# The second FFN's hi/lo split, cut into two steps: three plain slots, then four formed slots

## Chip, core and metric

The kernel runs on one core of a Trainium2 chip. The metric is the device time of one execution in microseconds (us). Beside the time of whole runs there is one profiled execution, with a trace of every engine: PE (TensorE matmuls) and PEld (its weight loads), DVE (VectorE), ACT (ScalarE), POOL (GpSimd), and SP, which only issues DMAs here.

## What is computed

```python
def _attn_ref(q, k, v, tau):                # 1 x 6016 x 256 each
    qn = q / (norm(q, axis=1) + 1e-06);  kn = k / (norm(k, axis=1) + 1e-06)
    s = kn.transpose(0, 2, 1) @ qn / tau    # 256 x 256
    a = softmax(s)
    return v @ a                            # 6016 x 256
def _moe_ref(x, w_in, w_out):               # FFN 1, d_model 256, d_ff 2048
    h = x @ w_in
    return (h * np.cos(h)) @ w_out
def _moe2_ref(x, w_in, w_out):              # FFN 2, the same sizes
    h = x @ w_in
    return (h * (1.0 / (1.0 + np.exp(-h)))) @ w_out     # silu(h)
# result: _moe2_ref(_moe_ref(_attn_ref(...)))
```

## The kernel before

**Stages.** After the attention's 256 x 256 matrix has been folded into FFN 1's first weights, the kernel is two FFNs, one after the other. Tokens go in 12 blocks (four of 512, then eight of 496), the hidden width of 2048 in 8 pairs of 128 rows. A *unit* is one FFN, one block b and one pair m: FFN 1 has 96 units, and then FFN 2 has 96. In names such as `h2_5_1` the numbers are FFN, block and pair.

**Precision.** Every matmul operand is kept as two parts, hi (the value rounded to fp32r) and lo (the rest), and a product takes three passes: hi·hi, hi·lo, lo·hi (`PASSES`).

**A unit of FFN 2.** PE computes h in 12 matmuls (L365) into one of two PSUM tiles `h`. ACT writes silu(h) into slots 0 to 3 of a tile `t` (L381): the 2 x 2 quarters of the block, two hidden halves by two token halves, each 128 x n/2. The second product is done by Strassen's scheme (Winograd's form), with seven products in place of eight. It needs four more slots, which DVE forms in `emit_cos` (L396 writes slots 4 and 5, L399 slot 6, L400 slot 7). `emit_split` then makes hi and lo of slots 1 to 7, one ACT copy (L414) and one DVE subtraction (L415). PE's second product is `emit_o2`: 21 matmuls (L465), seven products by three passes, into two PSUM tiles `o`.

```python
PRODUCTS = {"P1": (1, 1), "P2": (3, 3), "P3": (7, 2), "P4": (2, 7), "P5": (4, 4), "P6": (6, 6), "P7": (5, 5)}
BANKS = {
    "P1": (0, 0, 0), "P6": (0, 0, 1), "P7": (0, 1, 0), "P4": (0, 1, 1),
    "P5": (1, 0, 0), "P3": (1, 0, 1), "P2": (1, 1, 0),
}
```

The second number of a product is the slot of `t` that it reads, and the order of `BANKS` is the order in which PE works: P1 (slot 1), P6 (6), P7 (5), P4 (7) go into the first `o` tile, P5 (4), P3 (2), P2 (3) into the second. P1, P3 and P2 read plain slots, the others formed ones.

**End of a block.** `emit_out` takes a finished block out of PSUM: one ACT copy (L488, called q1 here) and seven DVE additions (L486). The third addition is the last that reads the first `o` tile, the seventh the last that reads the second. There are only two `o` tiles and a block holds both, so the next block's first product waits for these additions.

**Order.** The order on each engine is the order of the code, unit after unit (the loop at L528). Iteration i emits h of unit i, its silu, its forms, its split, and then the second product of unit i − 2 (`LAG = 2`); the second product of a block's last pair comes before the split (`early_o`), and with it `emit_out`, so that the additions of a block stand on DVE between the forms and the subtraction of the next block's unit m = 1. The tiles `t`, `hi`, `lo` and `h` have two buffers each: hi and lo of unit u can be written once the second product of unit u − 2 has read them.

Of the kernel before, what the change touches and what calls it, by code (L numbers as in the profile page):

```python
# [9 lines left out]
F32 = mybir.dt.float32  # L10
# [4 lines left out]
AF = mybir.ActivationFunctionType  # L15
ALU = mybir.AluOpType
# [22 lines left out]
NU = NS - 1  # L39
# [20 lines left out]
def attention_then_two_ffns(ctx: ExitStack, tc: tile.TileContext, qk, vT, tau, w_in1, w_out1, w_in2, w_out2, outT):  # L60
# [6 lines left out]
    nc = tc.nc  # L67
# [168 lines left out]
    for g, n in enumerate(GROUPS):  # L236
        c0 = sum(GROUPS[:g])
        t = ep.tile([P, GMAX, 2, C], F32, tag="qk", name=f"qk{g}", bufs=8)
# [47 lines left out]
    for a in range(CH):  # L286
        nc.vector.scalar_tensor_tensor(
            out=E[:, a], in0=S[:, a, :C], scalar=rk[:, a : a + 1], in1=rq, op0=ALU.mult, op1=ALU.mult
# [80 lines left out]
    def emit_first(u, hp):  # L369
        L, b, m = u  # L370
        n = BLOCKS[b][1]
        t = sc.tile([P, NS, HB], F32, tag="t", name=f"t{L}_{b}_{m}")
        if L == 1:
            t = t.rearrange("p s c -> p (s c)")[:, : 2 * TB].rearrange("p (s n) -> p s n", s=2)
            k = t.bitcast(I32)[:, :, :n]
            nc.scalar.activation(k, hp[:, :, :n], AF.Copy, scale=1.0 / TWO_PI, bias=0.25)  # L376
            nc.vector.scalar_tensor_tensor(  # L377
                out=t[:, :, :n], in0=k, scalar=-TWO_PI, in1=hp[:, :, :n], op0=ALU.mult, op1=ALU.add
            )
        else:  # L380
            nc.scalar.activation(  # L381
                t[:, :4].rearrange("p (s j) c -> p s j c", s=2)[:, :, :, : n // 2],
                hp[:, :, :n].rearrange("p s (j c) -> p s j c", j=2),
                AF.Silu,
            )
        return t
# [15 lines left out]
    def emit_split(u, t):  # L402
        L, b, m = u
        n = BLOCKS[b][1]
        hi = sc.tile([P, NU, HB], F32R, tag="hi", name=f"hi{L}_{b}_{m}")
        lo = sc.tile([P, NU, HB], F32R, tag="lo", name=f"lo{L}_{b}_{m}")
        if L == 1:
            hi, lo = [
                x.rearrange("p s c -> p (s c)")[:, : 2 * TB].rearrange("p (s n) -> p s n", s=2) for x in (hi, lo)
            ]  # L410
            w, z, x = hi[:, :, :n], lo[:, :, :n], t[:, :, :n]
        else:
            w, z, x = hi[:, :, : n // 2], lo[:, :, : n // 2], t[:, 1:, : n // 2]
        nc.scalar.activation(w, x, AF.Copy)  # L414
        nc.vector.tensor_tensor(out=z, in0=x, in1=w.bitcast(F32), op=ALU.subtract)  # L415
        return hi, lo

    def emit_o1(u, parts):
# [109 lines left out]
    for i in range(len(units) + LAG):  # L528
        if i < len(units):
# [13 lines left out]
            t = emit_first(u, hp)  # L543
        if pend is not None:
            parts[pend[0]] = emit_split(units[pend[0]], pend[1])
            pend = None
# [7 lines left out]
        if i < len(units):  # L554
            if L == 1:
                pend = (i, t)
            else:
                parts[i] = emit_split(u, t)
            if (L, b) == (1, 0):
                WO1.load()  # L560
                WO1.decode()
                if m >= NPAIR - 2:
                    WI2.load()
            if (L, b) in ((1, 1), (1, 2)) and m % 2 == 0:
                WI2.decode()
                WI2.load()
            if (L, b) == (1, 2) and m >= NPAIR - 2:
                WO2.load()
            if (L, b) in ((1, 3), (1, 4), (1, 5), (1, 6)) and m % 4 == 0:
                WO2.decode()  # L570
                WO2.load()
            if m == 2:
                if L == 1 and 1 <= b < NB - 1:
                    load_v(b + 1)
                elif (L, b) == (1, NB - 1):
                    load_x2(0)
                elif L == 2 and b < NB - 1:
                    load_x2(b + 1)
            if (L, b) == (1, NB - 1) and m % 2 == 1:
                fetch_wo2(HELD + m // 2)  # L580
# [32 lines left out]
```

## Time and profile before

| what | value |
|---|---|
| time, median of 3 runs | 1136.78 us (1136.54 to 1137.22) |
| the profiled execution: time, and its span | 1136.23 us, 1134.5 us |
| busy in the span: PE, PEld, DVE, ACT, POOL | 1093.4, 933.5, 835.9, 612.1, 207.0 us |
| mean granted TensorE clock | 0.995 |
| FFN 2, from its first h matmul to the end | 600.46 to 1134.5 us |

The span runs from the first to the last instruction; the time of the execution has 1.7 us more around it. "Idle before" in a row is the time that an engine stood still ahead of that instruction, with the instruction that ended it. [...]

### The profile page before, as it was taken

What the parts mean: (1) busy time and instruction counts of PE and PEld (TensorE: products, weight loads), DVE (VectorE), ACT (ScalarE), POOL (GpSimd) and SP (SyncE); (2) the same over time, 40 slices, a digit from 0 to 9 for tenths busy, and PEclk for the clock granted to TensorE, in tenths of its full rate; (3) what the DMA queues carried; (4) which work ended last, traced back from release to release, by engine and by line L of the source; (5) the groups of instructions that cost most, each with busy time, mean ns of one, the idle gap of its engine ahead of it and who ended that gap; (6) DMA issues with size and microseconds to landing.
All of it is one profiled execution on the core that took longest, in us unless ns stands there. A gap on an engine that the chain in (4) does not pass through costs nothing.

```text
span 1134.5 us, 14054 instructions
## 1 busy us (share of the span) xinstructions
PE 1093.4 (96%) x5724; PEld 933.5 (82%) x5724; DVE 835.9 (74%) x914; ACT 612.1 (54%) x582; POOL 207.0 (18%) x173
## 2 busy tenths in 40 slices
PE   8888999999999999999999999999999999999997
PEld 7746788888888888888888888988988988988986
DVE  6899988877887766677666677677677667676675
ACT  6555666656656555555554444544444444445443
POOL 2268565543543311011000000000000000000000
PEclk9999999999999999999999999999999999999999
DMA  9812222303133011011063011010110110110100
GB/s 356 283 47 83 94 75 93 111 19 106 52 135 108 38 49 54 1 55 54 1 235 106 1 57 52 5 55 18 38 54 9 47 54 1 55 55 1 55 18 19
DMA packets 31792, 77.97 MB, mean 69 GB/s; under 512 B 2416, under 2 KB 14704, under 8 KB 31728
## 3 DMA queue, kind: packets, MB, share of 16 engines
q1 hardware_dynamic: 31584, 76.83, 19.8%
q8 instruction: 45, 0.74, 0.3%
q10 hardware_dynamic: 144, 0.25, 0.1%
q14 instruction: 19, 0.16, 0.0%
HBM read 53.08 MB, written 23.99 MB: 68 GB/s over the span
## 4 chain that ended last, share of the span: by engine, by line
PE 75%; DVE 18%; ACT 5%; issue 1%; DMA 1%; SPq 0%; ACTq 0%; DVEq 0%
PE h L365 38%; PE o L425 22%; PE o L465 15%; DVE lo L415 6%; ACT hi L414 4%; DVE acc L256 2%; DVE t L396 2%; DVE t L399 1%; DVE t L400 1%; PE pw L323 1%; DMA qk<-qk_dram 1%; DVE t L377 1%; DVE q L486 1%; DVE t L393 1%; DVE wv_wo L129 1%
## 5 line engine op out<-in xcount | busy, mean ns | idle before, releaser
L415 DVE TENSOR_TENSOR lo<-t,hi 128x992 fp32r<-128x992 f32 (+3 forms) x192 | 324.0, 1687 | 156.7 <-ACT hi L414 156.7
L414 ACT ACTIVATE hi<-t 128x992 fp32r<-128x992 f32 (+3 forms) x192 | 260.0, 1354 | 267.3 <-DVE t L400 236.6
L465 PE MATMUL o<-hi,wo 128*128 128x248 f32 (+1 forms) x1344 | 241.7, 282 | 18.0 <-DVE ob L486 17.1
L465 PEld LDWEIGHTS o<-hi,wo 128*128 128x128 f32 x1344 | 212.3, 191 | 29.6 <-issue 21.6
L365 PE MATMUL h<-xhi,wa 128*128 128x496 f32 (+1 forms) x768 | 206.2, 391 | 3.0 <-DVE wa L331 3.0
L425 PE MATMUL o<-hi,wo 128*128 128x496 f32 (+1 forms) x768 | 205.9, 390 | 0.0
L377 DVE SCALAR_TENSOR_TENSOR t<-t,h 128x992 f32<-128x992 int32 (+1 forms) x96 | 115.0, 1198 | 106.5 <-ACT t L376 106.2
L465 PE MATMUL o<-lo,wo 128*128 128x248 f32 (+1 forms) x672 | 188.5, 281 | 2.6 <-DVE lo L415 2.6
L376 ACT ACTIVATE t<-h 128x992 int32<-128x992 f32 (+1 forms) x96 | 96.9, 1009 | 157.5 <-PE h L365 153.4
L365 PEld LDWEIGHTS h<-xhi,wa 128*128 128x128 f32 x768 | 144.3, 188 | 34.5 <-issue 4.3
L425 PEld LDWEIGHTS o<-hi,wo 128*128 128x128 f32 x768 | 144.4, 188 | 30.5
L392 ACT ACTIVATE t<-t,half_pi 128x992 f32<-128x992 f32 (+1 forms) x96 | 109.1, 1137 | 55.8 <-DVE t L377 55.8
L465 PEld LDWEIGHTS o<-lo,wo 128*128 128x128 f32 x672 | 128.0, 190 | 3.0 <-DVE lo L415 3.0
L425 PE MATMUL o<-lo,wo 128*128 128x496 f32 (+1 forms) x384 | 119.2, 392 | 6.2 <-DVE lo L415 6.2
L393 DVE TENSOR_TENSOR t<-h,t 128x992 f32<-128x992 f32 (+1 forms) x96 | 115.1, 1199 | 7.1 <-ACT t L392 1.2
L365 PE MATMUL h<-x2lo,wi_hi 128*128 128x496 f32 (+1 forms) x384 | 119.5, 393 | 0.0
L365 PE MATMUL h<-x2hi,wi_lo 128*128 128x496 f32 (+1 forms) x384 | 118.9, 391 | 0.0
L365 PE MATMUL h<-x2hi,wi_hi 128*128 128x496 f32 (+1 forms) x384 | 118.8, 391 | 0.0
L365 PE MATMUL h<-xlo,wa 128*128 128x496 f32 (+1 forms) x384 | 118.4, 390 | 0.0
L381 ACT ACTIVATE t<-h 128x992 f32<-128x992 f32 (+1 forms) x96 | 95.0, 989 | 2.9 <-PE h L365 2.8
L425 PEld LDWEIGHTS o<-lo,wo 128*128 128x128 f32 x384 | 71.6, 188 | 23.7 <-DVE lo L415 9.2
L365 PEld LDWEIGHTS h<-x2lo,wi_hi 128*128 128x128 f32 x384 | 72.3, 188 | 15.3
(88 smaller groups left out, 912.7 us busy)
## 6 DMA issues: line engine op xcount, KB each, us to landing
qk<-qk_dram SPq DMA_DIRECT2D x22, 512.0 KB, 7.2
raw_wo<-w_out_dram SPq DMA_DIRECT2D x16, 512.0 KB, 3.9
wo_dram<-stage SPq DMA_DIRECT2D x6, 896.0 KB, 4.5
wo<-wo_dram SPq DMA_DIRECT2D x6, 896.0 KB, 5.5
raw_w<-w_in_dram SPq DMA_DIRECT2D x8, 512.0 KB, 7.6
raw_wi<-w_in_dram SPq DMA_DIRECT2D x8, 512.0 KB, 3.8
vraw<-vT_dram SPq DMA_DIRECT2D x8, 496.0 KB, 5.4
xshi<-yhi SPq DMA_DIRECT2D x8, 496.0 KB, 4.0
```

The source lines that it names most:

```text
L256: nc.vector.tensor_tensor(out=acc[:, :n], in0=acc[:, :n], in1=sq[:, :n], op=ALU.add)
L365: nc.tensor.matmul(hp[:, s, :n], lhsT, rhs, start=(i == 0), stop=(i == len(todo) - 1))
L376: nc.scalar.activation(k, hp[:, :, :n], AF.Copy, scale=1.0 / TWO_PI, bias=0.25)
L377: nc.vector.scalar_tensor_tensor(out=t[:, :, :n], in0=k, scalar=-TWO_PI, in1=hp[:, :, :n], op0=ALU.mult, op1=ALU.add)
L381: nc.scalar.activation(t[:, :4].rearrange("p (s j) c -> p s j c", s=2)[:, :, :, : n // 2], hp[:, :, :n].rearrange("p s (j c) -> p s j c", ...
L392: nc.scalar.activation(t[:, :, :n], t[:, :, :n], AF.Sin, bias=half_pi)
L393: nc.vector.tensor_tensor(out=t[:, :, :n], in0=hp[:, :, :n], in1=t[:, :, :n], op=ALU.mult)
L396: nc.vector.tensor_tensor(out=t[:, 4:6, :c], in0=t[:, 0:1, :c].to_broadcast([P, 2, c]), in1=t[:, 1:3, :c], op=ALU.subtract)
L414: nc.scalar.activation(w, x, AF.Copy)
L415: nc.vector.tensor_tensor(out=z, in0=x, in1=w.bitcast(F32), op=ALU.subtract)
L425: nc.tensor.matmul(o[:, e, :n], wo1_at(i, f)[:, e * P : (e + 1) * P], parts[k][:, s, :n], start=(f == 0 and (i, k) == PASSES[0]), stop=(f ...
L465: nc.tensor.matmul(o[t][:, k, j, :c], wo2[m][:, w, wa_ - 1], parts[x][:, xb - 1, :c], start=(m == 0 and i == 0 and j == 0), stop=(m == NPA ...
```

## The change

For FFN 2 `emit_split` no longer works on seven slots at once. It emits a copy and a subtraction of slots 1 to 3, which silu writes, and then a copy and a subtraction of slots 4 to 7, which the forms write. The operations, their engines and their operands are otherwise the same; FFN 1 has one step as before. Line numbers after it move by three (L414 and L415 are L417 and L418, L465 is L468, L486 and L488 are L489 and L491).

```diff
@@ emit_split
         else:
-            w, z, x = hi[:, :, : n // 2], lo[:, :, : n // 2], t[:, 1:, : n // 2]
-        nc.scalar.activation(w, x, AF.Copy)
-        nc.vector.tensor_tensor(out=z, in0=x, in1=w.bitcast(F32), op=ALU.subtract)
+            some = [
+                (hi[:, a:z, : n // 2], lo[:, a:z, : n // 2], t[:, 1 + a : 1 + z, : n // 2]) for a, z in ((0, 3), (3, NU))
+            ]
+        for w, z, x in some:
+            nc.scalar.activation(w, x, AF.Copy)
+            nc.vector.tensor_tensor(out=z, in0=x, in1=w.bitcast(F32), op=ALU.subtract)
         return hi, lo
```

ACT before, at the border from block 4 to block 5 (units 5_1 to 5_3), with the engines whose semaphores an instruction waits for; "Activation" is ACT itself:

```order
L381 ACTIVATE t2_5_1_6063<-h2_5_1_6050 128x4x248 [waits PE_49]
L488 ACTIVATE q4_6089<-o2_4_0_5769 128x248 [waits PE_49]
L414 ACTIVATE hi2_5_1_6100<-t2_5_1_6063 128x7x248 [waits DVE_49,PE_49,Activation_49]
L381 ACTIVATE t2_5_2_6117<-h2_5_2_6104 128x4x248 [waits PE_49]
L414 ACTIVATE hi2_5_2_6122<-t2_5_2_6117 128x7x248 [waits DVE_49,PE_49,Activation_49]
L381 ACTIVATE t2_5_3_6166<-h2_5_3_6153 128x4x248 [waits PE_49]
```

The same place of ACT with the change:

```order
L381 ACTIVATE t2_5_1_6145<-h2_5_1_6132 128x4x248 [waits PE_49]
L491 ACTIVATE q4_6171<-o2_4_0_5839 128x248 [waits PE_49]
L417 ACTIVATE hi2_5_1_6182<-t2_5_1_6145 128x3x248 [waits PE_49,Activation_49]
L417 ACTIVATE hi2_5_1_6182<-t2_5_1_6145 128x4x248 [waits DVE_49]
L381 ACTIVATE t2_5_2_6201<-h2_5_2_6188 128x4x248 [waits PE_49]
L417 ACTIVATE hi2_5_2_6206<-t2_5_2_6201 128x3x248 [waits PE_49,Activation_49]
L417 ACTIVATE hi2_5_2_6206<-t2_5_2_6201 128x4x248 [waits DVE_49]
L381 ACTIVATE t2_5_3_6252<-h2_5_3_6239 128x4x248 [waits PE_49]
```

One copy has become two. The copy of three slots no longer waits for DVE; it still waits for PE, the last matmul that reads the buffer (unit u − 2). The copy of four waits for DVE alone, for the L400 of its own unit.

DVE with the change, at the same border (the seven L489 are `emit_out`'s additions); before, one subtraction `128x7x248`, waiting for ACT, stood in the place of the two L418 rows, and the other rows were the same:

```order
L489 TENSOR_TENSOR q4_6171<-q4_6171,o2_4_0_5839 128x248 [waits Activation_49]
L489 TENSOR_TENSOR q4_6171<-q4_6171,o2_4_0_5839 128x248 [waits DVE_49]
L489 TENSOR_TENSOR ob4_6172<-q4_6171,o2_4_0_5839 128x248 [waits DMAHW7_49,DVE_49]
L489 TENSOR_TENSOR ob4_6172<-q4_6171,o2_4_1_5840 128x248 [waits PE_49]
L489 TENSOR_TENSOR q4_6171<-q4_6171,o2_4_1_5840 128x248 [waits DVE_49]
L489 TENSOR_TENSOR ob4_6172<-q4_6171,o2_4_1_5840 128x248 [waits DVE_49]
L489 TENSOR_TENSOR ob4_6172<-q4_6171,o2_4_1_5840 128x248
L418 TENSOR_TENSOR lo2_5_1_6183<-t2_5_1_6145,hi2_5_1_6182 128x3x248 [waits Activation_49]
L418 TENSOR_TENSOR lo2_5_1_6183<-t2_5_1_6145,hi2_5_1_6182 128x4x248 [waits Activation_49]
L396 TENSOR_TENSOR t2_5_2_6201<-t2_5_2_6201 128x2x248 [waits Activation_49]
L399 TENSOR_TENSOR t2_5_2_6201<-t2_5_2_6201 128x248 [waits DVE_49]
```

Nothing has moved past anything else on DVE: forms, additions, then the two subtractions in place of one.

PE with the change, the first eight of the 21 matmuls of unit 5_1's second product; before, the rows that wait were only the first and the third:

```order
L468 MATMUL o2_5_0_6216<-hi2_5_1_6182,wo2_1_530 128x248 [waits Activation_49]
L468 MATMUL o2_5_0_6216<-hi2_5_1_6182,wo2_1_530 128x248
L468 MATMUL o2_5_0_6216<-lo2_5_1_6183,wo2_1_530 128x248 [waits DVE_49]
L468 MATMUL o2_5_0_6216<-hi2_5_1_6182,wo2_1_530 128x248 [waits Activation_49]
L468 MATMUL o2_5_0_6216<-hi2_5_1_6182,wo2_1_530 128x248
L468 MATMUL o2_5_0_6216<-lo2_5_1_6183,wo2_1_530 128x248 [waits DVE_49]
L468 MATMUL o2_5_0_6216<-hi2_5_1_6182,wo2_1_530 128x248 x2
```

PE's matmuls and their order are as before; P6, the second product, now waits by itself for the copy and the subtraction of the four slots.

## Rows read from the trace of the kernel before

**Rows 1.** The page's part 4, shares of the chain that ended last.
```profile
PE 75%; DVE 18%; ACT 5%; issue 1%; DMA 1%; SPq 0%; ACTq 0%; DVEq 0%
```

**Rows 2.** Windows: stretch, its length, busy time per engine, clock, DMA share, GB/s.
```profile
160.00:605.96 445.96, 445.96 (x1965) 368.91 (x1964) 332.83 (x294) 266.45 (x268) 124.07 (x101) 1.00 0.22 74
...
702.47:706.56 4.09, 4.09 (x21) 4.09 (x22) 3.99 (x7) 1.34 (x2) 0.00 (x0) 0.58 0.46 137
...
833.38:876.31 42.93, 41.19 (x264) 37.21 (x265) 29.62 (x40) 20.58 (x18) 0.00 (x0) 1.00 0.11 36
```

**Rows 3.** Who waited for whom, 640 to 1130 us: total, times, longest.
```profile
ACT hi L414 <- DVE t L400: 221.6, 79, 3.7
DVE lo L415 <- ACT hi L414: 143.8, 79, 2.1
...
PE o L465 <- DVE ob L486: 17.1, 10, 1.8
```

**Rows 4.** DVE's timeline at a block's border: start, us, instruction, idle before.
```profile
825.18 0.67 DVE L396 TENSOR_TENSOR t<-t 128x496 f32<-128x496 f32 x1
...
826.34 0.42 DVE L400 TENSOR_TENSOR t<-t 128x248 f32<-128x248 f32 x1
828.56 1.97 DVE L415 TENSOR_TENSOR lo<-t,hi 128x1736 fp32r<-128x1736 f32 x1 [1.80 <-ACT hi L414]
830.44 0.67 DVE L396 TENSOR_TENSOR t<-t 128x496 f32<-128x496 f32 x1
...
831.93 0.85 DVE L486 TENSOR_TENSOR q<-q,o 128x248 f32<-128x248 f32 x2
832.82 0.73 DVE L486 TENSOR_TENSOR ob<-q,o 128x248 f32<-128x248 f32 x2
...
834.03 0.73 DVE L486 TENSOR_TENSOR ob<-q,o 128x248 f32<-128x248 f32 x2
```

**Rows 5.** ACT's timeline at the same border.
```profile
826.87 1.66 ACT L414 ACTIVATE hi<-t 128x1736 fp32r<-128x1736 f32 x1 [2.72 <-DVE t L400]
828.43 0.98 ACT L381 ACTIVATE t<-h 128x992 f32<-128x992 f32 x1
829.30 0.37 ACT L488 ACTIVATE q<-o 128x248 f32<-128x248 f32 x1
```

**Rows 6.** PE's timeline in FFN 2: first matmuls of first and second products.
```profile
614.25 0.40 PE L465 MATMUL o<-hi,wo 128*128 128x256 f32 x2
...
635.37 0.41 PE L465 MATMUL o<-hi,wo 128*128 128x256 f32 x2
...
790.41 0.47 PE L465 MATMUL o<-hi,wo 128*128 128x248 f32 x2 [1.60 <-DVE ob L486]
...
823.66 0.61 PE L365 MATMUL h<-x2hi,wi_hi 128*128 128x496 f32 x2
...
826.38 0.39 PE L465 MATMUL o<-hi,wo 128*128 128x248 f32 x2
...
828.76 0.61 PE L365 MATMUL h<-x2hi,wi_hi 128*128 128x496 f32 x2
...
833.38 0.47 PE L465 MATMUL o<-hi,wo 128*128 128x248 f32 x2 [1.74 <-DVE ob L486]
...
1090.98 0.47 PE L465 MATMUL o<-hi,wo 128*128 128x248 f32 x2 [1.74 <-DVE ob L486]
```

**Rows 7.** Timelines of ACT and DVE at FFN 1's last unit.
```profile
604.38 1.02 ACT L414 ACTIVATE hi<-t 128x992 fp32r<-128x992 f32 x1
...
605.43 1.19 DVE L415 TENSOR_TENSOR lo<-t,hi 128x992 fp32r<-128x992 f32 x1 [2.89 <-ACT hi L414]
```

**Rows 8.** The kernel's end, PE and ACT.
```profile
1116.72 0.39 PE L465 MATMUL o<-hi,wo 128*128 128x248 f32 x2
...
1125.85 0.38 PE L465 MATMUL o<-lo,wo 128*128 128x248 f32 x1 [1.51 <-DVE lo L415]
...
1127.93 0.38 ACT L488 ACTIVATE q<-o 128x248 f32<-128x248 f32 x1 [4.13 <-PE o L465]
```

More of the change, by code (lines that the diff above doesn't have):

```diff
@@ L410, in emit_split @@
             ]
-            w, z, x = hi[:, :, :n], lo[:, :, :n], t[:, :, :n]
+            some = [(hi[:, :, :n], lo[:, :, :n], t[:, :, :n])]
         else:
-            w, z, x = hi[:, :, : n // 2], lo[:, :, : n // 2], t[:, 1:, : n // 2]
-        nc.scalar.activation(w, x, AF.Copy)
-        nc.vector.tensor_tensor(out=z, in0=x, in1=w.bitcast(F32), op=ALU.subtract)
+            some = [
[4 more added lines that the diff above has]
+            nc.vector.tensor_tensor(out=z, in0=x, in1=w.bitcast(F32), op=ALU.subtract)
         return hi, lo
```

## Prediction

> **What bounds the kernel now.** I began with PE by stage. In FFN 1 (160 to 606 us) PE is busy 445.96 of 445.96 us; in a block of FFN 2 it is busy 41.19 of 42.93 us [rows 2]. FFN 1 has no idle time of PE to give, and the change leaves it alone, so only FFN 2 is looked at. There PE is busy but not the bound: the chain that ended last runs 18% through DVE and 5% through ACT [rows 1], and the waits of FFN 2 show a pair that hand work to each other, ACT's copy waiting for DVE's forms (221.6 us) and DVE's subtraction waiting for the copy (143.8 us) [rows 3]. Such waits cost nothing by themselves. They matter if their loop is longer than PE's unit.
>
> PE's unit: from the h product at 823.66 us to the next at 828.76 is 5.10 us, 2.72 for h and 2.38 for the second product [rows 6]. The loop of DVE and ACT: forms from 825.18 to 826.76 (1.58), handover 0.11, copy 1.66, handover 0.03, subtraction 1.97, and the next forms begin at 830.44 [rows 4, 5]. That is 5.26 us, 0.16 more than PE's. So DVE falls behind PE in each unit. PE doesn't feel it within a block, since it uses hi and lo two units later. It feels it at the border, where the additions that free the `o` tiles stand on DVE behind the late forms: they begin at 831.93, PE can start at 833.38, 1.74 us idle [rows 4, 6]. Ten such waits make 17.1 us [rows 3].
>
> A check that the loop is what sets the pace: the additions run from 831.93 to 834.76 and the subtraction follows, so a border unit takes about 1.6 + 2.8 + 1.9 = 6.2 us, and 7 × 5.26 + 6.2 = 43.0. The measured block is 42.93 [rows 2]; PE's own work would be 8 × 5.10 = 40.8.
>
> **The change part by part.** Sizes for blocks of 496. The copy of four slots is 128 x 992, and so is its subtraction: FFN 1's last unit has both shapes, 1.02 on ACT and 1.19 on DVE [rows 7]. The step of three slots is 128 x 744. On DVE it lies between 128 x 496 (0.67) and 128 x 992 (1.19) [rows 4, 7], halfway 0.93. On ACT 1736 columns take 1.66 and 992 take 1.02 [rows 5, 7]; on that line 744 take 0.81. So the split costs DVE 0.93 + 1.19 − 1.97 = 0.15 us more per unit and ACT 0.81 + 1.02 − 1.66 = 0.17 more.
>
> What it takes off the loop: between forms and the next forms there now stand only the handover, the copy of four (1.02), the handover and the subtraction of four (1.19); the copy of three is done earlier, and the subtraction of three (0.93) fills the 1.16 us in which DVE waits for the second copy. The loop is 1.58 + 0.11 + 1.02 + 0.03 + 1.19 − 0.08 (the next DVE instruction starts that much before the end of the one before) = 3.85 us. That is 1.25 under PE's 5.10. PE sets the pace.
>
> One wait keeps "right behind silu" from being literal. The copy of three writes hi, which the second product of unit u − 2 must have read. Let h of unit u end at T on PE. With 0.2 for a handover from PE (estimate; the restart after the third addition, 832.82 plus half of the pair to 833.38, takes about 0.15 [rows 4, 6]): silu T+0.2 to 1.2, forms to T+2.8, second product of u − 2 done at T+2.4, so the copy of three runs T+2.6 to 3.4, the copy of four to 4.4, the subtractions 3.4 to 4.4 and 4.45 to 5.65. The next silu is due at T+5.3 and the next forms at T+6.3: spare 0.9 on ACT, 0.65 on DVE. By the same sum the kernel before keeps DVE until T+6.55, some 0.2 too late, which is the 0.16 of the loop. hi and lo of u are wanted at T+10.2.
>
> The border. T is the end of h of the new block's m = 1; the last product of the old block runs T to T+2.4, h of m = 2 to T+5.1. q1 is taken to need the first tile's 12 of the 21 matmuls: T+1.6 to 1.95. The additions begin when the forms end, T+2.8; the third is done 1.3 later (831.93 to about 833.2) and PE may write the first `o` tile at T+4.25. It wants it at T+5.1. All seven take 2.83, free at T+5.75; PE wants the second tile 12 matmuls of 0.114 later, T+6.5. Both fit, with 0.85 and 0.7 to spare, so the wait goes and nothing takes its place. The two subtractions end at T+7.7, the next forms start 1.4 late, and at 3.85 a unit against 5.10 that is made up in two units.
>
> What PE gets back, from its own rows [rows 6]. From the first product of block 0 to that of block 4, 614.25 to 790.41, is 176.16 us. A unit of 512 takes (635.37 − 614.25)/4 = 5.28; 32 units, less 0.08 for each of the three h products that are already 496 wide, make 168.7. Gain 7.4. [...] From 790.41 to 1090.98 is 300.57, against 56 × 5.10 = 285.6. Gain 15.0. The restart behind 1090.98 gives 0.2 more: 1116.72 − 1090.98 = 25.7 for five units of 5.10 [rows 6, 8]. Sum 22.6.
>
> The end. T is now 1116.72, the end of the last h. Before, the last products wait for the late split three times, 1.51 at the last, and q1 comes at T+11.2, with the end 6.6 behind it [rows 8]. After: two products to T+4.8, P1 to 5.1, P6's hi passes to 5.35, its lo pass waits for the last subtraction to 5.7, seven matmuls to 6.5, q1 at 6.7, the end at T+13.2. Before it was T+17.8. Gain 4.6.
>
> Sum 27.2. The profiled execution has 1136.23, so 1109.0; the median of the runs shown is 0.55 higher, so 1109.6. I say **1109.3 us** (span about 1107.3).
>
> PE itself: two more matmuls per unit carry a wait. The rows of before show 2.38 us for 21 matmuls with two waits, 0.114 each, and no step that a wait would explain [rows 6]; I take nothing, and bound it by ACT's and DVE's shortest handover, 0.03 per wait, 192 waits, 5.8 us.
>
> [...] A 744-wide and a 992-wide instruction cost 0.15 and 0.17 us more than one of 1736 [rows 4, 5, 7]. [...]
>
> **Rivals.**
> 1. *The borders keep part of the wait.* The additions still stand behind the forms, and the spare is 0.85 and 0.7. If silu, forms or q1 come 1.4 us later than my handovers say, PE still waits 0.7 at each of 11 borders: 7.7 us, 1117. For it: the sum of five handovers is an estimate. Against it: each is 0.03 to 0.2 in the rows. It decides from 0.7 of lateness on.
> 2. *Satisfied waits cost PE time.* 5.8 us as bounded above, 1115.
> 3. *The second copy comes too late.* The change would not do what it says if the copy of four also waited for the subtraction of three, so that the engines take turns again. The loop is then 1.58 + 0.11 + 0.93 + 0.05 + 1.02 + 0.03 + 1.19 = 4.9, and a border unit, with 2.83 of additions, 7.7: 7 × 4.9 + 7.7 = 42.0 a block. That is still over PE's 40.8; of the 2.1 us that a border loses now it gives back 0.9. With 11 borders and the end about 11 us, 1125. Against it: in the order on ACT that copy waits for DVE at its own L400, which stands ahead of the subtraction.
> 4. *Slower.* The two steps don't overlap: working side by side slows both engines, or the copy of three is so late that nothing is done ahead, and the loop keeps all its parts and gains 0.15 + 0.17. Then 0.32 × 96 = 31 us, 1167. It decides from a loop of 5.26 on. Against it: DVE's lengths lie on one line whether ACT works or not. From 0.67 at 496 columns and 1.19 at 992 (ACT idle behind 605.40) 1736 should take 0.67 + 1240 × 0.52/496 = 1.97, and the subtraction at 828.56, with silu and q1 beside it, took 1.97 [rows 4, 5, 7]. And PE held a clock of 1.00 over 446 us without a pause beside both engines [rows 2].
>
> **Chances.** The forecast 0.75, its own range 1106 to 1112 (handovers, the end, 0.5 between runs). Rival 1 0.10, rival 2 0.05, rival 3 0.04, rival 4 0.04, and 0.02 for a loop between rivals 3 and 4, near the old 5.26, which would leave the time where it is. The range reaches to the first two rivals, 1106 to 1118. No change means within 0.2%, 2.3 us, about what a measurement of this kernel can tell from it. Faster: the forecast and rivals 1 to 3, 0.94; same 0.02; slower 0.04.
>
> **What would show it.** Right: the waits of PE for the additions gone from the list, blocks of 496 at 40.8 us, ACT's copies waiting for PE and for DVE by turns, silu at 0.2 behind h, clock 1.00 through FFN 2, two copies of about 0.81 and 1.02 and two subtractions of 0.93 and 1.19. Wrong: PE idle at the borders still (rival 1), second products longer than 2.38 us without idle time ahead of them (rival 2), a copy of four that starts behind the subtraction of three (rival 3), or longer DVE and ACT instructions (rival 4).

## The result and the profile after

The changed kernel takes 1109.56 us (median of 4 runs, 1109.37 to 1110.12) against 1136.93 us for the kernel before (4 runs): ratio 0.976, 95% interval 0.9743 to 0.9777. Its profiled execution took 1109.38 us with a span of 1107.6; the forecast was 1109.3 with a span of 1107.3.

The page's part 4, the chain that ended last, shares by engine; it answers to [rows 1]:

```profile
PE 89%; DVE 8%; DMA 1%; ACT 1%; SPq 0%; issue 0%; DVEq 0%; ACTq 0%
```

DVE fell from 18% of the chain to 8%, ACT from 5% to 1%. These are shares of the whole span. From 600 us on, the lines of the chain before add up to 21% for DVE and 9% for ACT, those of the chain after to 1% and under 1%; nearly all that is left of the 8% lies ahead of FFN 2. Windows (length, busy time of PE, PEld, DVE, ACT, POOL, clock, DMA share, GB/s) of FFN 2 up to its last h product, and of one block of 496:

```profile
600.00:1094.70 494.70, 494.70 (x3134) 447.03 (x3133) 376.92 (x557) 272.16 (x300) 0.00 (x0) 1.00 0.12 39
829.15:870.01 40.86, 40.86 (x266) 37.19 (x264) 31.30 (x48) 22.49 (x25) 0.00 (x0) 1.00 0.12 39
```

PE is busy without a gap for 494.70 us, at a clock of 1.00, and a block takes 40.86 us where it took 42.93 [rows 2]. Who waited for whom in FFN 2, the five largest (total, times, longest):

```profile
ACT hi L417 <- PE o L468: 119.7, 94, 1.7
ACT t L381 <- PE h L365: 90.7, 94, 2.1
DVE t L396 <- ACT t L381: 61.2, 82, 0.9
DVE lo L418 <- ACT hi L417: 49.1, 85, 2.9
ACT hi L417 <- DVE t L400: 7.2, 12, 1.6
```

The direction has turned. Before, from 640 to 1130 us, ACT waited for DVE for 221.6 us and DVE for ACT for 143.8 [rows 3]; now ACT waits for PE, both ahead of silu and ahead of the copy of three, and the wait of PE for the additions (17.1 us) is gone. The largest wait in the list costs nothing: it is ACT's, which is busy for 272.16 of the 494.70 us, and PE has no gap.

DVE's timeline at the same border as in [rows 4] (`x2` is two instructions in a row, shown with the first one's shape):

```profile
816.22 0.42 DVE L400 TENSOR_TENSOR t<-t 128x248 f32<-128x248 f32 x1
817.22 2.11 DVE L418 TENSOR_TENSOR lo<-t,hi 128x744 fp32r<-128x744 f32 x2 [0.58 <-ACT hi L417]
820.16 0.68 DVE L396 TENSOR_TENSOR t<-t 128x496 f32<-128x496 f32 x1 [0.83 <-ACT t L381]
...
821.66 0.85 DVE L489 TENSOR_TENSOR q<-q,o 128x248 f32<-128x248 f32 x2
822.55 0.74 DVE L489 TENSOR_TENSOR ob<-q,o 128x248 f32<-128x248 f32 x2
...
823.76 0.73 DVE L489 TENSOR_TENSOR ob<-q,o 128x248 f32<-128x248 f32 x2
824.42 2.03 DVE L418 TENSOR_TENSOR lo<-t,hi 128x744 fp32r<-128x744 f32 x2
```

ACT there, to be held against [rows 5]:

```profile
816.36 1.75 ACT L417 ACTIVATE hi<-t 128x744 fp32r<-128x744 f32 x2 [1.33 <-PE o L468]
819.13 1.00 ACT L381 ACTIVATE t<-h 128x992 f32<-128x992 f32 x1 [1.02 <-PE h L365]
820.49 0.38 ACT L491 ACTIVATE q<-o 128x248 f32<-128x248 f32 x1 [0.36 <-PE o L468]
821.45 1.75 ACT L417 ACTIVATE hi<-t 128x744 fp32r<-128x744 f32 x2 [0.59 <-PE o L468]
```

And PE's second products, with those of [rows 6] that they answer to at 614.25, 790.41, 1090.98 and, for the end, [rows 8]:

```profile
614.57 0.40 PE L468 MATMUL o<-hi,wo 128*128 128x256 f32 x2
...
783.17 0.39 PE L468 MATMUL o<-hi,wo 128*128 128x248 f32 x2
...
818.93 0.39 PE L468 MATMUL o<-hi,wo 128*128 128x248 f32 x2
...
824.03 0.39 PE L468 MATMUL o<-hi,wo 128*128 128x248 f32 x2
...
1069.15 0.39 PE L468 MATMUL o<-hi,wo 128*128 128x248 f32 x2
...
1094.71 0.39 PE L468 MATMUL o<-hi,wo 128*128 128x248 f32 x2
```

The last h of the new block's m = 1 ends at 818.93. Silu starts 0.20 later, the forms are done and the additions begin 2.73 later, the third ends at about 822.96, and PE, which may then write the first `o` tile, comes to it at 824.03 without having stood still.

The time came from these places. Blocks 0 to 3, first product to first product: 783.17 − 614.57 = 168.60 in place of 176.16, 7.6 us. The next seven: 1069.15 − 783.17 = 285.98 in place of 300.57, 14.6. From there to the last h 25.56 in place of 25.74, 0.2. From the last h to the end 1107.6 − 1094.71 = 12.9 in place of 17.8, 4.9. FFN 2's first product is 0.3 later. Sum 26.9, the difference of the spans (1134.5 − 1107.6).

### The profile page after: what moved, and what is told of

It reads as the page before. It is cut to its first block, busy times and chain, and to the rows that moved or that the text cites. A ratio compares the mean times of both kernels' runs of the same rounds, so it can differ in the third digit from the quotient of the medians.

```text
span 1107.6 us, 14245 instructions
## 1 busy us (share of the span) xinstructions
PE 1085.0 (98%) x5724; PEld 928.1 (84%) x5724; DVE 857.2 (77%) x1010; ACT 634.0 (57%) x678; POOL 207.7 (19%) x173
## 4 chain that ended last, share of the span: by engine, by line
PE 89%; DVE 8%; DMA 1%; ACT 1%; SPq 0%; issue 0%; DVEq 0%; ACTq 0%
PE h L365 45%; PE o L428 22%; PE o L468 21%; DVE acc L256 2%; DVE lo L418 1%; PE pw L323 1%; DMA qk<-qk_dram 1%; DVE t L377 1%; DVE t L393 1%; DVE wv_wo L129 1%; DVE wv_wo L133 0%; DVE wv_wo L130 0%; SPq L240 0%; DVE w L133 0%; DVE wa L331 0%
## 5 line engine op out<-in xcount | busy, mean ns | idle before, releaser
L418 DVE TENSOR_TENSOR lo<-t,hi 128x992 fp32r<-128x992 f32 (+3 forms) x288 | 340.3, 1188 | 49.1 <-ACT hi L417 49.1
L417 ACT ACTIVATE hi<-t 128x992 fp32r<-128x992 f32 (+3 forms) x288 | 270.3, 966 | 127.6 <-PE o L468 119.7
L468 PE MATMUL o<-hi,wo 128*128 128x248 f32 (+1 forms) x1344 | 236.8, 278 | 0.0
L468 PEld LDWEIGHTS o<-hi,wo 128*128 128x128 f32 x1344 | 210.6, 188 | 7.6
L468 PE MATMUL o<-lo,wo 128*128 128x248 f32 (+1 forms) x672 | 186.6, 278 | 0.1
L468 PEld LDWEIGHTS o<-lo,wo 128*128 128x128 f32 x672 | 126.2, 188 | 0.3 <-DVE lo L418 0.3
L396 DVE TENSOR_TENSOR t<-t 128x496 f32<-128x496 f32 (+1 forms) x96 | 65.3, 680 | 61.2 <-ACT t L381 61.2
```

The source lines that it names most:

```text
L396: nc.vector.tensor_tensor(out=t[:, 4:6, :c], in0=t[:, 0:1, :c].to_broadcast([P, 2, c]), in1=t[:, 1:3, :c], op=ALU.subtract)
L468: nc.tensor.matmul(o[t][:, k, j, :c], wo2[m][:, w, wa_ - 1], parts[x][:, xb - 1, :c], start=(m == 0 and i == 0 and j == 0), stop=(m == NPA ...
```

## Experiments

The theory is that two loops run side by side in FFN 2, PE's unit of 5.10 us and the loop of DVE and ACT, and that the longer one sets the length of a block: seven rounds of DVE and ACT and the longer one at the border, or PE's 8 × 5.10 = 40.8 us. The change brings the second from 5.26 to about 3.85. Its rivals are that each of the two splits simply gives its share (A), that the wait of PE at the border is the cause and not a symptom (B), that the early copy of the plain slots is what counts (C), and that DVE's work counts in proportion (D).

**Two copies, one subtraction.** From the changed kernel:

```diff
         for w, z, x in some:
             nc.scalar.activation(w, x, AF.Copy)
-            nc.vector.tensor_tensor(out=z, in0=x, in1=w.bitcast(F32), op=ALU.subtract)
+        if L == 2:
+            some = [(hi[:, :, : n // 2], lo[:, :, : n // 2], t[:, 1:, : n // 2])]
+        for w, z, x in some:
+            nc.vector.tensor_tensor(out=z, in0=x, in1=w.bitcast(F32), op=ALU.subtract)
```

Expected: 

> The two copies of the changed kernel, but one subtraction of seven slots behind them. Theory (the loop of DVE and ACT must be shorter than PE's unit of 5.10 us): the loop is 1.58 forms + 0.11 + 1.03 copy of four + 0.03 + 1.97 - 0.08 = 4.64, under 5.10, so the borders stay free of waits and only the end is later, by 1.0 (P1's lo pass waits for the whole subtraction): 1110.5 us. Rival A (each of the two splits gives its share, the gain goes with what each shortens: of the loop's 1.41 this one takes 0.62, the other the rest): 0.44 of 27.4, about 1125.

Measured: 1110.46 us, ratio to before 0.977 (0.9754 to 0.9787). The list of PE's waits in FFN 2 has one entry, in the last unit; PE's timeline:

```profile
1100.93 0.38 PE L471 MATMUL o<-lo,wo 128*128 128x248 f32 x1 [1.18 <-DVE lo L421]
```

DVE's forms behind a border, where DVE catches up and its loop can be seen:

```profile
826.19 0.67 DVE L396 TENSOR_TENSOR t<-t 128x496 f32<-128x496 f32 x1
...
830.75 0.67 DVE L396 TENSOR_TENSOR t<-t 128x496 f32<-128x496 f32 x1
```

The loop is 4.56, and with 6.13 at the border (826.19 − 820.06, forms to forms) a block of DVE and ACT would take 38.1, under PE's 40.8. All of the gain at the borders is there with half of the change, so rival A is out. As far as the traces show, the second split is worth only the end.

**One copy, two subtractions.** From the changed kernel:

```diff
+        whole = [(hi[:, :, : n // 2], lo[:, :, : n // 2], t[:, 1:, : n // 2])] if L == 2 else some
-        for w, z, x in some:
+        for w, z, x in whole:
             nc.scalar.activation(w, x, AF.Copy)
+        for w, z, x in some:
             nc.vector.tensor_tensor(out=z, in0=x, in1=w.bitcast(F32), op=ALU.subtract)
```

Expected: 

> The two subtractions of the changed kernel behind one copy of seven slots. Theory: the copy holds DVE as before and the subtractions cost 0.15 more than one, so the loop is 1.58 + 0.11 + 1.66 + 0.03 + 2.12 - 0.08 = 5.42, a border unit 0.1 to 0.15 longer than the 6.2 of before, a block 1.3 longer than 42.93; with 11 blocks 14 us over the kernel before: 1151 us. Rival A (each split gives its share): under 1137. Rival B (PE's own waits at the border are what counts, not the loop): within 3 us of 1137, since the additions still stand where they stood.

Measured: 1142.81 us, ratio 1.0052 (1.0035 to 1.0069). Slower, as the theory has it, but by 6 us and not by 14. DVE's timeline in the middle of a block, and PE's at two borders in a row:

```profile
815.63 2.03 DVE L420 TENSOR_TENSOR lo<-t,hi 128x744 fp32r<-128x744 f32 x2 [1.80 <-ACT hi L418]
...
820.96 2.03 DVE L420 TENSOR_TENSOR lo<-t,hi 128x744 fp32r<-128x744 f32 x2 [1.80 <-ACT hi L418]
```

```profile
836.50 0.48 PE L470 MATMUL o<-hi,wo 128*128 128x248 f32 x2 [2.29 <-DVE ob L491]
879.98 0.47 PE L470 MATMUL o<-hi,wo 128*128 128x248 f32 x2 [0.72 <-DVE ob L491]
923.45 0.76 PE L470 MATMUL o<-hi,wo 128*128 128x248 f32 x2 [2.28 <-DVE ob L491]
```

The size was off, not the mechanism. Where both subtractions are ready when DVE comes to them, 0.93 and 1.19 take 2.03, not 2.12, so the loop is 820.96 − 815.63 = 5.33 in place of my 5.42. A block is 43.47 (923.45 − 879.98), and 7 × 5.33 + 6.2 is 43.5. With 0.54 more in each of 11 blocks the kernel is 6 us longer, which is the result. Rivals A and B had it at or under the kernel before, or within 3 us; both are out.

The two borders show a second thing. PE stood still for 2.29 us at one and for 0.72 at the next, and the blocks are equally long to 0.01 us. Windows behind the two borders:

```profile
836.50:840.60 4.10, 4.10 (x23) 4.02 (x24) 4.00 (x8) 1.29 (x2) 0.00 (x0) 0.69 0.44 132
...
879.98:884.00 4.02, 4.02 (x28) 3.76 (x29) 3.92 (x8) 1.29 (x2) 0.00 (x0) 1.00 0.44 131
```

Behind the long wait the granted clock was 0.69 and PE did 23 matmuls in 4.1 us, behind the short one 1.00 and 28. Between the first two borders PE was busy for 42.76 us, between the next two for 41.19: the 1.6 us that it lost at the lower clock were taken off its next wait. In these blocks a PE that wasn't the bound ran slowly for a while and nothing changed. The kernel before has such a pair too. Behind the slow matmuls at 702.47 [rows 2] PE comes to the next border so late that the `o` tiles are all but free, and its rows there leave 0.1 us:

```profile
745.79 0.63 PE L365 MATMUL h<-x2lo,wi_hi 128*128 128x512 f32 x2
746.52 0.48 PE L465 MATMUL o<-hi,wo 128*128 128x256 f32 x2
```

**The formed slots first.** One line of the changed kernel:

```diff
-for a, z in ((0, 3), (3, NU))
+for a, z in ((3, NU), (0, 3))
```

Expected: 

> Two steps in the other order, the formed slots first, the plain ones second, so that nothing is copied before the forms are done. Theory: the copy of three runs beside the subtraction of four, the loop is 1.58 + 0.11 + 1.03 + 0.03 + 1.19 + 0.93 - 0.08 = 4.79, under 5.10, no waits of PE at the borders, and the end is later by 0.9 (P1's lo pass waits for the last subtraction): 1110.4 us. Rival C (the gain comes from copying the plain slots ahead of the forms): most of it gone, 1130 or more.

Measured: 1110.33 us, ratio 0.9769 (0.9753 to 0.9785). The two largest waits of FFN 2, PE's only wait, and DVE's forms behind a border:

```profile
ACT hi L417 <- DVE t L400: 174.8, 96, 3.1
DVE lo L418 <- ACT hi L417: 100.1, 84, 2.9
```

```profile
1100.70 0.38 PE L468 MATMUL o<-lo,wo 128*128 128x248 f32 x1 [0.86 <-DVE lo L418]
```

```profile
826.28 0.67 DVE L396 TENSOR_TENSOR t<-t 128x496 f32<-128x496 f32 x1
...
830.97 0.67 DVE L396 TENSOR_TENSOR t<-t 128x496 f32<-128x496 f32 x1
```

ACT waits for DVE for 174.8 us and DVE for ACT for 100.1, about three quarters and two thirds of what the page of the kernel before has for its whole run (236.6 and 156.7), and yet the time is that of the changed kernel to within 0.8 us. So it is not the early copy (rival C) and not the sum of such waits that counts, but whether seven loops and a border stay under PE's 40.8. Here the loop is 4.69, and 7 × 4.69 + 6.2 is 39.0.

**The additions ahead of the forms, split in one step.** In the main loop of the kernel before:

```diff
+        v = units[i - LAG] if i >= LAG else None
+        early_o = v is not None and v[2] == NPAIR - 1
+        first = early_o and v[0] == 2
+        if first:
+            emit_o(v, parts.pop(i - LAG))
         if i < len(units):
             emit_cos(u, hp, t)
-        v = units[i - LAG] if i >= LAG else None
-
-        early_o = v is not None and v[2] == NPAIR - 1
-        if early_o:
+        if early_o and not first:
             emit_o(v, parts.pop(i - LAG))
```

Expected: 

> The kernel before, with the additions of a finished block ahead of the forms of the next block's unit m = 1 and not behind them; the split in one step. Theory: the loop stays 5.26, and a border unit grows from 6.2 to 2.83 + 1.58 + 0.11 + 1.66 + 0.03 + 1.97 = 8.1, since the additions no longer run beside the copy; a block takes 7 x 5.26 + 8.1 = 44.9, 2.0 more in each of 11: about 1158 us, with PE waiting for lo or hi in place of the additions. Rival B (the wait of PE for the additions at the border is the whole of it, and freeing the o tiles 1.6 us earlier takes away nearly all of 1.74): about 1114.

Measured: 1157.26 us, ratio 1.0177 (1.0161 to 1.0192). DVE at a border, and PE's waits there:

```profile
839.58 0.85 DVE L486 TENSOR_TENSOR q<-q,o 128x248 f32<-128x248 f32 x2
...
842.34 0.67 DVE L396 TENSOR_TENSOR t<-t 128x496 f32<-128x496 f32 x1
...
845.71 1.97 DVE L415 TENSOR_TENSOR lo<-t,hi 128x1736 fp32r<-128x1736 f32 x1 [1.80 <-ACT hi L414]
847.60 0.67 DVE L396 TENSOR_TENSOR t<-t 128x496 f32<-128x496 f32 x1
```

```profile
841.03 0.47 PE L465 MATMUL o<-hi,wo 128*128 128x248 f32 x2 [1.44 <-DVE ob L486]
847.73 0.38 PE L465 MATMUL o<-lo,wo 128*128 128x248 f32 x1 [1.01 <-DVE lo L415]
885.86 0.47 PE L465 MATMUL o<-hi,wo 128*128 128x248 f32 x2 [1.44 <-DVE ob L486]
```

Freeing the `o` tiles earlier in DVE's order made the kernel 20 us slower. The border unit takes 847.60 − 839.58 = 8.02 where it took about 6.2, because the additions no longer hide behind ACT's copy, and the block grows to 885.86 − 841.03 = 44.83 (forecast 44.9). The wait for the additions is shorter (1.44 in place of 1.74) and a wait for lo has come beside it. That is rival B's answer: the place where PE waits is a symptom.

**More work for DVE: the first form twice, and three times, in each unit.** The result is the same; from the changed kernel, with 2 or 3 in the range (the rest of the statement only moves in):

```diff
+            for _ in range(2):
+                nc.vector.tensor_tensor(
-            nc.vector.tensor_tensor(
```

Expected, twice: 

> The changed kernel with the first form (0.68 us on DVE) done twice in every unit of FFN 2, with the same result: 96 x 0.7 = 67 us more work for DVE. Theory (a threshold): the loop is 3.85 + 0.70 = 4.55, still under PE's 5.10; at the border the additions are 0.7 later, and the spare there was 0.9 for the first o tile and 0.76 for the second, so PE waits for 0.1 at the most: 1109.6 to 1111.5 us, 0.7 of it at the end. Rival D (no threshold, DVE's work counts in proportion, as the 21 us that DVE and ACT got busier by in the change would): 10 us or more.

Expected, three times: 

> The same with the first form three times: 134 us more work for DVE. Theory: the loop is 3.85 + 1.40 = 5.25, over 5.10, and a border unit 2.98 forms + 2.83 additions + 2.03 subtractions - 0.1 = 7.75; a block takes 7 x 5.25 + 7.75 = 44.5 in place of 40.9, 3.6 more in each of 11, and 1.4 at the end: about 1150 us, with PE waiting for the additions at the borders again, some 3 us each time, and perhaps lower clocks behind these waits. Rival D (in proportion): twice what the single repeat costs. Rival E (no bound by the loop at all, only the last unit's latency counts): 1111.

Measured: twice 1109.88 us, ratio 0.977 (0.9756 to 0.9785); three times 1149.24 us, ratio 1.0121 (1.0104 to 1.0138). PE's waits, first of the one (its only one), then two borders of the other; and the forms of both on DVE, of the first while it catches up:

```profile
1100.83 0.38 PE L469 MATMUL o<-lo,wo 128*128 128x248 f32 x1 [0.38 <-DVE lo L419]
```

```profile
839.29 0.76 PE L469 MATMUL o<-hi,wo 128*128 128x248 f32 x2 [2.84 <-DVE ob L490]
883.32 0.47 PE L469 MATMUL o<-hi,wo 128*128 128x248 f32 x2 [1.53 <-DVE ob L490]
```

```profile
827.31 1.38 DVE L397 TENSOR_TENSOR t<-t 128x496 f32<-128x496 f32 x2
...
829.18 0.42 DVE L401 TENSOR_TENSOR t<-t 128x248 f32<-128x248 f32 x1
...
831.80 1.38 DVE L397 TENSOR_TENSOR t<-t 128x496 f32<-128x496 f32 x2
```

```profile
819.33 2.09 DVE L397 TENSOR_TENSOR t<-t 128x496 f32<-128x496 f32 x3
...
824.53 2.09 DVE L397 TENSOR_TENSOR t<-t 128x496 f32<-128x496 f32 x3
```

The first repeat of the form, 67 us of work by the forecast, cost nothing that can be measured; the second cost 39 us. The pages have DVE busy for 857.2, 915.1 and 973.7 us with one form, two and three, so each repeat made it busier by 58 to 59. With two forms the loop is 831.80 − 827.31 = 4.49, and with 6.90 at the border (827.31 − 820.41) a block would take 38.3, under PE's 40.8. With three the loop is 824.53 − 819.33 = 5.20, and with 7.61 at the border (an estimate: the 6.90 with two forms, and 0.71 for the third) a block takes 44.0; the measured one is 44.03. The bound lies between, as the theory says. Rivals D and E (1111 us for three forms) are out.

No run has a block of DVE and ACT between 39.0 and 42.9 us, so the place of the bound is not shown more closely than that. By the sum a loop just under 5.10 would not be enough: 7 × 5.10 and 6.2 at the border make 41.9.

**The changed kernel again.** Expected: 

> The changed kernel once more, beside the kernel before on the same chip, so that differences of about 1 us can be read against it: 1109.6 us.

Measured beside the two last: 1109.75 us, ratio 0.9768 (0.9754 to 0.9783). The kernels with one subtraction, with the formed slots first and with the form twice are 0.1 to 0.7 us longer in the median, less than the 2.3 us that can be told apart. The first two ran on another chip, on which the kernel before also took 0.7 longer; the ratios are 0.977, 0.9769 and 0.977 for 0.9768 here. That their ends are later is read from the trace alone. None of them beats the change.

## Why the prediction was right, point by point

- **The bound.** That DVE and ACT set the pace of FFN 2 and PE does not was right: it foretold the sign of all six variants, and lengthening the loop brought the waits back at the same place.
- **The loop after the change.** The forecast was 3.85 us. In the changed kernel it can't be seen, since PE is longer, but from 4.49 with one more form at about 0.71 it is 3.78. The other loops came out 0.05 to 0.1 under my sums too (4.56 for 4.64, 4.69 for 4.79, 5.33 for 5.42, 4.49 for 4.55, 5.20 for 5.25). Two terms were too long. For 4.69 and 5.33 it is the pair of subtractions, 2.03 to 2.04 and not 2.12: I had counted the overlap of one instruction with the next only once in a loop. For the others it is the handover from the last form to the copy. I had taken 0.11 from the copy of seven [rows 4, 5]; where the copy of three goes ahead on ACT, the copy of four starts 0.02 to 0.04 behind the form (in the changed kernel at 827.97, behind 827.94). With the formed slots first it is an estimated 0.10: 1.16 us of idle DVE between the form and the subtraction, less 1.03 for the copy and 0.03 for the handover. That copy of seven waits for three engines and this copy of four for DVE alone; whether that is the reason was not tested.
- **The cost of splitting.** For DVE I had 0.15 us per unit. The lengths add up to that (0.93 + 1.19 − 1.97), but the loop pays only 0.07 if both instructions are ready (2.03 for the pair, with 5.33 − 5.26 = 0.07 for the loop). For ACT the forecast was 0.81 and 1.02; the groups show 0.83 and 1.02, and the pair together took 1.75. The busy time grew with the split: in the pages' rows the subtractions went from 324.0 to 340.3 us and the copies from 260.0 to 270.3. The engines as a whole are busier by more, DVE by 21 us (857.2 for 835.9) and ACT by 22 (634.0 for 612.1), but that is not all the split's. Silu, for one, used to begin 0.10 before the copy ahead of it ended (826.87 + 1.66 against 828.43 [rows 5]) and now waits for h, which makes an estimated 96 × 0.10 = 9.6 us on ACT. The kernel is 27 us faster.
- **The wait of the copy of three for the second product of unit u − 2** was there as said: 94 times, 119.7 us, and free. The copy starts 2.52 behind h (forecast 2.6).
- **The border.** Forecast spare 0.85 us for the first `o` tile; it is 824.03 − 822.96 − 0.15 = 0.92. Nothing took the place of the waits that went, and one form more per unit (0.7 us) still fitted.
- **The sums.** Borders and restarts 22.6 forecast, 7.6 + 14.6 + 0.2 = 22.4 measured; the end 4.6 forecast, 4.9 measured; the start of FFN 2, 0.3 later, was not in the sum.
- **The clock.** Behind 1.8 us of idle PE [rows 3] the 21 matmuls from 702.47 took 4.09 us at a granted clock of 0.58 [rows 2], inside the stretch that gave the 7.4 us. That gain was taken from the whole length of the stretch and is right, but the slow clock was not a part of it: DVE and ACT set the pace, and the experiment with one copy shows such a stretch being taken off the next wait. In the kernel before it is the same: the block with the slow matmuls took 44.05 us, the one ahead of it 44.33 (from 658.14). The border after the slow one is at 746.52, and there the wait was too short to be listed (the rows stand with that experiment), which is also why ten waits are listed for 11 borders.
- **The reading of [rows 1].** The prediction took 18% and 5% for FFN 2; they are shares of the whole span. From 600 us on it was 21% and 9%, so the conclusion stands.
- **The signs.** The lengths, the clock and silu's 0.20 came as listed. ACT's copies did not wait for PE and DVE by turns: the copy of three waited for PE 94 times, the copy of four for DVE only 12 times. By the prediction's own times it could not be otherwise, since the forms end at T+2.8 and the copy of three at T+3.4.
- **The rivals.** Waits kept at the borders: none. Satisfied waits on PE: a unit of 496 still takes 5.10 (824.03 − 818.93), with four waits in place of two. A late second copy: ruled out by the rows of ACT. Slower: the prediction let that begin at a loop of 5.26, and that is not the right mark. With the form three times the loop is 5.20 and the kernel is 13 us slower than before, because its border unit is about 7.61. The block decides: 43.5, 44.8 and 44.0 in the three slower variants, 42.9 before.

## What to carry to other kernels

Add up, for each set of engines that hand work to each other, the length of one round, waits for each other included, over a whole period (here a block with its border), and compare it with the same round of the busiest engine. In these runs the longer one set the time: PE's 40.8 us a block where DVE and ACT add up to 39.0 or less, and their 42.9 to 44.8 where they add up to more, with PE busy for 41.19 of 42.93. The split shortened that round, and was worth only what was left of the gap to PE's: about 2.1 us in a block of 42.93, some 1.1 of it from seven loops that are 0.16 too long and 1.0 from the border. Behind that, a further 0.7 us per unit was free to spend.

## What the hardware showed that was not expected

- Two DVE subtractions of 0.93 and 1.19 us take 2.03 when both are ready, 0.09 less than their sum; with the second released just as the first ended, 2.11 to 2.12.
- With one copy and two subtractions, where PE wasn't the bound, time lost at a lower granted clock was free: the two borders had 2.29 and 0.72 us of idle PE, and granted clocks of 0.69 and 1.00 behind them, in blocks of 43.48 and 43.47 us.
